# Even DFT tables ahead of the odd ones, and half of the odd ones issued from ScalarE

## The chip, the cores and the metric

The kernel runs on one core of a Trainium2 chip. The metric is the device time of one execution in microseconds (us): the median over several timed runs. Beside these there is one profiled execution, from which every row of the profile comes.

Engines are named as in the profile: PE (TensorE's matmuls), PEld (its weight loads), DVE (VectorE), ACT (ScalarE), POOL (GpSimd) and SP (SyncE, which computes nothing here and issues DMAs). SPq and ACTq are the DMA-issuing instructions of SP and ScalarE. L259 is line 259 of the kernel.

## The reference

`x` has shape 8 x 3136 x 256. All is float32 at the interface; the weights arrive as 64-bit floats, which the kernel narrows itself.

```python
X = np.fft.fft(x, axis=1)           # over the 3136 positions
X = np.fft.fft(X, axis=2)           # over the 256 features
x = X.real                          # float32

h  = np.maximum(x @ w_in, 0.0)      # w_in: 256 x 1024
hp = h padded with one zero row before and after each sequence
conv_out = conv_w[0] * hp[:, 0:S] + conv_w[1] * hp[:, 1:S+1] + conv_w[2] * hp[:, 2:S+2]
gate = 1 / (1 + np.exp(-conv_out))
out  = (h * gate) @ w_out           # w_out: 1024 x 256
```

## The kernel before

**Stages.** The Fourier transform over positions is made of matmuls with tables of cosines and sines. Symmetry is used first: `x[n]` and its mirror positions, and the quarters of the sequence, are added and subtracted on VectorE (the "fold", lines 156 to 194), so that the matmuls contract over 98 or 99 partitions only. The even output frequencies need the *even tables* (`tabs[0]`, tile `tab2`: cosine and sine, four columns of the fold, 393 frequencies each, 1.2 MB); the odd frequencies need the *odd tables* (`tabs[1]`, tile `tab4`: cosine and sine, 196 frequencies each for two columns, 0.3 MB) and, for the other two columns, the even tables again, with `w` scaled by a *turn* (`turn`, a cosine and a sine per partition, line 286). The transform over features is folded into `w_in` on PE (`G`, line 717). Then the FFN runs in steps of one sequence, one of four chunks of frequencies and one of eight blocks of 128 hidden units: two products on PE, ReLU sums and the convolution's taps on DVE and ACT, sigmoid on ACT, the gate on POOL and DVE, and the product with `w_out` on PE, which collects over the eight blocks.

**Order.** The order of the instructions on each engine is written out by hand. Sequence 0 is transformed alone at the start (the run-up); the transforms of sequences 1 to 7 are spread over the FFN steps of the sequence before. The change touches the run-up only.

**The run-up, as far as it matters.**

- *x of sequence 0* comes in two halves (`load_ops`, from line 109): one plain transfer from SP (line 118), four mirrored gathers from POOL (line 131), and for the second half three single-row transfers from ScalarE (line 125). A transfer is held back by a trick: POOL writes one element of the destination (`memset`, line 117) behind earlier work in its queue, and the transfer has to wait for that write.
- *Turn tables*: four transfers of 4-byte elements from ScalarE (line 286). Behind them ScalarE computes `turn[:, 2]` (line 697), which waits for them.
- *Odd tables* (`load_odd`, lines 268 to 280): for each of cosine and sine two transfers of 48 rows (one for the even and one for the odd partitions), one of two rows and one of the last row; eight in all from SP, held by a memset at line 698 that stands in POOL's queue behind the eight gathers.
- *Even tables* (`load_even`, lines 254 to 266): two transfers of 48 partitions, one of two, one of one, from SP behind the odd tables.
- Then, from SP too: the four blocks of `w_in` (line 651, tile `raw`) with the feature tables `dm` between them.
- *ScalarE* makes the scaled copies `rt` of the fold (`scaled`, line 216; four when the first half of x is folded, four when the second is), corrects a row of the odd tables (`mend_row`, line 294) and writes the negated and mirrored copies of both odd tables (`mirror_tables`, line 300).
- *PE* runs eight matmuls of 512 columns whose results nobody reads (`keep_on`, tiles `pb` and `pa`), then four units of the odd frequencies in turns, a quarter of each at a time (tiles `po<-tab,w` with the odd tables, `po<-tab,rt` with the even ones), then the units of the even frequencies.
- *VectorE* narrows the first block of `w_in` (lines 617 to 635) after the fold, then combines PE's results (lines 383 to 416).

A product takes 98 partitions of a table, and 99 where the fold's last column (`q == 3`) brings an extra row. In that extra row the odd tables hold zeros for the column with index 0 and a row of values for the column with index 1.

```python
for i in range(4):
    for j, u in enumerate(odds):
        u.part(i)
```

`dma_start` only issues; completion is reported through a semaphore, on which the reading instruction waits. The framework gives each transfer issued from SP or ScalarE one of eight such counters in turn, and makes a transfer wait until the one before it on the same counter has landed.

Of the kernel before, what the change touches and what calls it, by code (L numbers as in the profile page):

```python
# [30 lines left out]
NQ = 8  # L31
# [5 lines left out]
def kernel(  # L37
# [10 lines left out]
    nc = tc.nc  # L48
# [5 lines left out]
    NP = Q4 // NQ  # L54
    KR = NP + 1
    HQ = NQ // 2
    NK = M + 1
    HE = Q4 // 2 + 1
    HO = Q4 // 2
    QO = HO // 2  # L60
# [179 lines left out]
    tabs = [const.tile([P, 2, HQ, HE], F32, name="tab2"), const.tile([P, 4, 2, QO], F32, name="tab4")]  # L240
# [10 lines left out]
    MR = NP // 2 // 16 * 16  # L251
    assert NP == 2 * MR + 2

    def load_even():

        to = tabs[0].rearrange("p s q i -> p s (q i)")
        n = HQ * HE
        for i in range(2):
            nc.sync.dma_start(out=to[i:2 * MR:2], in_=dft_seq[0:MR, 0:2, HQ * i:HQ * (i + 1)]  # L259
                              .rearrange("p s q i -> p s (q i)"))  # L260
        nc.sync.dma_start(out=to[2 * MR:NP], in_=bass.AP(
            tensor=dft_seq.tensor, offset=dft_seq.offset + MR * 4 * NQ * HE,
            ap=[[n, 2], [NQ * HE, 2], [1, n]]))
        nc.sync.dma_start(out=to[NP:KR], in_=bass.AP(
            tensor=dft_seq.tensor, offset=dft_seq.offset + (NP * 4 * NQ - HQ + 2) * HE,
            ap=[[n, 1], [NQ * HE, 2], [1, n]]))

    def load_odd(eng):

        def at_(p, s, q):  # L270
            return dft_seq.offset + ((p * 4 + 2 + s) * NQ + q) * HE
        for s in range(2):
            for i in range(2):
                eng.dma_start(out=tabs[1][i:2 * MR:2, s], in_=bass.AP(
                    tensor=dft_seq.tensor, offset=at_(0, s, HQ * i + 1),
                    ap=[[4 * NQ * HE, MR], [2 * HE, 2], [1, QO]]))
            eng.dma_start(out=tabs[1][2 * MR:NP, s], in_=bass.AP(
                tensor=dft_seq.tensor, offset=at_(MR, s, 1), ap=[[HQ * HE, 2], [2 * HE, 2], [1, QO]]))
            eng.dma_start(out=tabs[1][NP:KR, s], in_=bass.AP(
                tensor=dft_seq.tensor, offset=at_(NP, s, -1), ap=[[2 * HE, 1], [2 * HE, 2], [1, QO]]))  # L280

    def load_turn(eng):

# [411 lines left out]

    load_turn(nc.scalar)
    act(turn[0:NP, 2], turn[0:NP, 1], AF.Copy, scale=-1.0)
    nc.gpsimd.memset(tabs[1][0:1, 0, 0, 0:1], 0.0)
    load_odd(nc.sync)
    load_even()  # L700
    w_in[0].load(nc.sync)
    nc.sync.dma_start(out=dm, in_=dft_dim[:, :, 0:2])
    for i in (1, 2, 3):
# [209 lines left out]
    p = psd.tile([P, 512], F32, name="pd", tag="pd")  # L913
# [200 lines left out]
```

## Time and profile before

| what | us |
|---|---|
| timed runs, median of 3 | 1200.08 (1199.71 to 1200.8) |
| the profiled execution's own time | 1194.98 |
| its span, first to last instruction | 1193.2 |
| PE busy | 1152.5 |
| DVE busy | 1134.9 |
| ACT busy | 899.6 |
| first 100 us: PE busy, DVE busy | 74.95, 79.83 |
| from 100 us on, of 1093.0: PE busy, DVE busy | 1077.55, 1055.03 |

A row of the profile's timeline gives start, duration, engine, line, operation, destination<-source, shapes and count, and in brackets the time the engine stood idle before it and what ended that. Rows of the chain of waits give start, duration and what the end of the program hung on at that time; followed back from the last instruction, the chain runs through the run-up. Times are from the start of the span. The mean of a core's granted TensorE clock over the span was 0.995 of full speed.

### The profile page before, as it was taken

What the parts mean: (1) busy time and instruction counts of PE and PEld (TensorE: products, weight loads), DVE (VectorE), ACT (ScalarE), POOL (GpSimd) and SP (SyncE); (2) the same over time, 40 slices, a digit from 0 to 9 for tenths busy, and PEclk for the clock granted to TensorE, in tenths of its full rate; (3) what the DMA queues carried; (4) which work ended last, traced back from release to release, by engine and by line L of the source; (5) the groups of instructions that cost most, each with busy time, mean ns of one, the idle gap of its engine ahead of it and who ended that gap; (6) DMA issues with size and microseconds to landing.
All of it is one profiled execution on the core that took longest, in us unless ns stands there. A gap on an engine that the chain in (4) does not pass through costs nothing.

```text
span 1193.2 us, 15532 instructions
## 1 busy us (share of the span) xinstructions
PE 1152.5 (97%) x4836; PEld 890.9 (75%) x4836; DVE 1134.9 (95%) x1693; ACT 899.6 (75%) x1937; POOL 405.5 (34%) x476
## 2 busy tenths in 40 slices
PE   3899999999999999999999999999999999999998
PEld 1766777678876787777778777777778777777776
DVE  6799999999999999999999999999999998999996
ACT  2377767787777777778786877888787777888885
POOL 5235524524253423344423242242312233222222
PEclk9899999999999999999999999999999999999999
DMA  7622232311032120211121020310001100110001
GB/s 179 200 17 75 77 41 74 89 40 57 13 108 59 55 61 30 73 54 61 47 75 51 15 81 27 89 47 27 27 16 39 32 27 28 47 34 27 27 27 31
DMA packets 70723, 65.16 MB, mean 55 GB/s; under 512 B 28563, under 2 KB 58535, under 8 KB 70641
## 3 DMA queue, kind: packets, MB, share of 16 engines
q1 hardware_dynamic: 64583, 51.05, 15.4%
q0 software_dynamic: 5120, 12.85, 3.7%
q8 instruction: 38, 0.62, 0.2%
q10 hardware_dynamic: 938, 0.28, 0.1%
q14 instruction: 44, 0.36, 0.1%
HBM read 38.40 MB, written 25.74 MB: 54 GB/s over the span
## 4 chain that ended last, share of the span: by engine, by line
PE 72%; DVE 16%; issue 4%; ACT 4%; DMA 2%; POOL 1%; SPq 0%; DVEq 0%; ACTq 0%; POOLq 0%
PE po L92 46%; PE pb L92 11%; PE pa L92 10%; DVE g L806 7%; PE pd L92 5%; DVE h L795 3%; DVE g L830 2%; POOL xh L131 1%; DMA tab<-dft_seq_dram 1%; ACT nb L784 1%; ACT g L821 1%; DMA out_dram<-os 1%; ACT os L854 1%; DVE w L194 1%; DMA xh<-in_x_dram 0%
## 5 line engine op out<-in xcount | busy, mean ns | idle before, releaser
L92 PE MATMUL po<-wout,g 128*128 128x256 f32 x3072 | 709.8, 381 | 10.8 <-DVE g L830 10.2
L92 PEld LDWEIGHTS po<-wout,g 128*128 128x128 f32 x3072 | 577.6, 190 | 166.3 <-DVE g L830 48.4
L806 DVE SCALAR_TENSOR_TENSOR g<-h,cw,g 128x770 f32<-128x770 f32 (+1 forms) x512 | 564.8, 1103 | 4.1 <-ACT g L801 0.9
L829 POOL TENSOR_TENSOR g<-g,h 128x385 f32<-128x385 f32 (+2 forms) x256 | 265.1, 1036 | 727.5 <-ACT g L821 550.2
L821 ACT ACTIVATE g<-g 128x385 f32<-128x385 f32 (+4 forms) x512 | 245.2, 531 | 167.9 <-DVE g L806 167.2
L784 ACT ACTIVATE nb<-pb 128x386 f32<-128x386 f32 (+2 forms) x494 | 218.6, 497 | 68.3 <-PE pb L92 66.8
L795 DVE CUSTOM_DVE_ANT_0 h<-pa,nb 128x386 f32<-128x386 f32 (+2 forms) x503 | 260.0, 556 | 1.7 <-POOL h L762 1.7
L801 ACT ACTIVATE g<-h,cw 128x770 f32<-128x770 f32 (+1 forms) x256 | 244.2, 954 | 0.0
L92 PE MATMUL pb<-qt,G 127*128 127x387 f32 (+2 forms) x512 | 214.6, 500 | 1.8 <-ACT nb L784 0.8
L92 PE MATMUL pa<-pt,G 128*128 128x387 f32 (+2 forms) x512 | 212.2, 495 | 0.3 <-ACT pa L748 0.3
L748 ACT ACTIVATE pa<-eb,ge 128x387 f32<-128x387 f32 (+2 forms) x256 | 155.3, 607 | 1.6 <-DVE h L795 1.0
L92 PEld LDWEIGHTS pa<-pt,G 128*128 128x128 f32 x512 | 97.2, 190 | 74.4 <-issue 18.1
L830 DVE TENSOR_TENSOR g<-g,h 128x385 f32<-128x385 f32 (+2 forms) x256 | 148.2, 579 | 3.4 <-ACT g L821 3.4
L131 POOL DMA_INDIRECT xh<-in_x_dram,idx x64 | 101.9, 1592 | 13.0 <-issue 9.7
L92 PE MATMUL pd<-tab,w 98*128 98x197 f32 (+2 forms) x448 | 98.5, 318 | 1.0 <-DVE w L194 1.0
L92 PEld LDWEIGHTS pb<-qt,G 127*128 127x128 f32 x512 | 91.1, 190 | 8.1 <-ACT G L717 2.0
L92 PEld LDWEIGHTS pd<-tab,w 98*128 98x128 f32 (+1 forms) x448 | 81.9, 191 | 10.8 <-issue 1.6
L854 ACT COPY os<-po 128x256 f32<-128x256 f32 x196 | 57.5, 398 | 8.7 <-DMA out_dram<-os 5.3
L156 DVE TENSOR_TENSOR xh<-xh 98x1020 f32<-98x1020 f32 (+1 forms) x32 | 39.4, 1234 | 4.0 <-DMA xh<-in_x_dram,idx 4.0
L167 DVE TENSOR_TENSOR xh<-xh 98x1024 f32<-98x1024 f32 (+1 forms) x32 | 39.9, 1246 | 0.1
L178 POOL COPY w<-xh 98x4 f32<-98x4 f32 (+1 forms) x32 | 26.9, 842 | 7.3 <-DVE xh L172 3.7
L193 DVE TENSOR_TENSOR w<-xh 98x508 f32<-98x508 f32 (+1 forms) x32 | 22.3, 698 | 0.1
(136 smaller groups left out, 376.9 us busy)
## 6 DMA issues: line engine op xcount, KB each, us to landing
out_dram<-os SPq DMA_DIRECT2D x192, 128.0 KB
xh<-in_x_dram SPq DMA_DIRECT2D x16, 784.0 KB
eb<-ed SPq DMA_DIRECT2D x16, 193.5 KB
raw<-in_moe_w_in_dram SPq DMA_DIRECT2D x4, 512.0 KB
raw<-in_moe_w_out_dram SPq DMA_DIRECT2D x1, 2048.0 KB
eb<-ed SPq DMA_DIRECT2D x8, 209.0 KB
eb<-ed SPq DMA_DIRECT2D x7, 193.0 KB
tab<-dft_seq_dram SPq DMA_DIRECT2D x2, 589.5 KB
```

The costliest lines, as they stand in the source:

```text
L92: nc.tensor.matmul(o, l, r, start=start, stop=stop, skip_group_check=True)
L131: nc.gpsimd.indirect_dma_start(out=xh[b, h][0:NP, 7 - m].rearrange("p q d -> p (q d)"), out_offset=None, in_=bass.AP(tensor=x.tensor, offs ...
L167: vt(flat(to, to + 2), flat(0, 2), flat(2, 4), op=op)
L748: act(pa[s][:, 0:n], eb[b, c], AF.Copy, scale=ge[:, f:f + 1])
L784: act(nb[s][:, i, cols], p[:, cols], AF.Copy, scale=-1.0 if i else 1.0)
L795: nc.vector._custom_dve(TENSOR_ADD_SAT, out=to, in0=a[:, cols], in1=c[:, i, cols], s0=BIG, s1=0.0)
L801: act(gs[s], hs[s][:, 0:n], AF.Copy, scale=cw[:, 0, s[2]:s[2] + 1])
L806: stt(out=g, in0=h[:, k:k + n], scalar=cw[:, k, f:f + 1], in1=g, op0=ALU.mult, op1=ALU.add)
L821: act(gs[s][:, c], gs[s][:, c], AF.Sigmoid)
L829: gt(g[:, p], g[:, p], h[:, p], op=ALU.mult)
L830: vt(g[:, v], g[:, v], h[:, v], op=ALU.mult)
L854: nc.scalar.copy(out=osb[:, j % 2], in_=pt[:, j % 2])
```

## The change

The order of the table loads in SP's queue is turned round: the even tables come right behind the second half of x, held by a memset of `tabs[0]`; the odd tables follow. `load_odd` now loads one of the two odd tables per call: the sine (`s = 1`) is issued from ScalarE's queue, behind the computation of `turn[:, 2]`, and the cosine (`s = 0`) from SP's queue behind the even tables. The extra row of both odd tables comes in one transfer with the sine, for the column with index 1 alone; the zeros of the column with index 0 are written by POOL (three partitions from 96 on; the loads then overwrite the first two of these). Seven transfers of odd tables take the place of eight, and three memsets that of one. What is computed stays the same.

```diff
-    def load_odd(eng):
-
-        def at_(p, s, q):
+    def load_odd(eng, s):
+
+        def at_(p, q):
             return dft_seq.offset + ((p * 4 + 2 + s) * NQ + q) * HE
-        for s in range(2):
-            for i in range(2):
-                eng.dma_start(out=tabs[1][i:2 * MR:2, s], in_=bass.AP(
-                    tensor=dft_seq.tensor, offset=at_(0, s, HQ * i + 1),
-                    ap=[[4 * NQ * HE, MR], [2 * HE, 2], [1, QO]]))
-            eng.dma_start(out=tabs[1][2 * MR:NP, s], in_=bass.AP(
-                tensor=dft_seq.tensor, offset=at_(MR, s, 1), ap=[[HQ * HE, 2], [2 * HE, 2], [1, QO]]))
-            eng.dma_start(out=tabs[1][NP:KR, s], in_=bass.AP(
-                tensor=dft_seq.tensor, offset=at_(NP, s, -1), ap=[[2 * HE, 1], [2 * HE, 2], [1, QO]]))
+        for i in range(2):
+            eng.dma_start(out=tabs[1][i:2 * MR:2, s], in_=bass.AP(
+                tensor=dft_seq.tensor, offset=at_(0, HQ * i + 1), ap=[[4 * NQ * HE, MR], [2 * HE, 2], [1, QO]]))
+        eng.dma_start(out=tabs[1][2 * MR:NP, s], in_=bass.AP(
+            tensor=dft_seq.tensor, offset=at_(MR, 1), ap=[[HQ * HE, 2], [2 * HE, 2], [1, QO]]))
+        if s:
+            eng.dma_start(out=tabs[1][NP:KR, 0:2, 1], in_=bass.AP(
+                tensor=dft_seq.tensor, offset=dft_seq.offset + ((NP * 4 + 2) * NQ + 1) * HE,
+                ap=[[HE, 1], [NQ * HE, 2], [1, QO]]))
...
     load_turn(nc.scalar)
     act(turn[0:NP, 2], turn[0:NP, 1], AF.Copy, scale=-1.0)
-    nc.gpsimd.memset(tabs[1][0:1, 0, 0, 0:1], 0.0)
-    load_odd(nc.sync)
+    nc.gpsimd.memset(tabs[0][0:1, 0, 0, 0:1], 0.0)
+    nc.gpsimd.memset(tabs[1][0:1, 1, 0, 0:1], 0.0)
+    nc.gpsimd.memset(tabs[1][96:KR, 0:2, 0], 0.0)
+    load_odd(nc.scalar, 1)
     load_even()
+    load_odd(nc.sync, 0)
     w_in[0].load(nc.sync)
```

## The prediction

> **What bounds the kernel now.** I read the page first, then the chain of waits over the first 120 us, the queue waits of SP, the timeline of the first 60 us, and last the windows and the DMA view around one gap. The span, and the busy time of each engine:
>
> ```profile
> span 1193.2 us, 15532 instructions
> PE 1152.5 (97%) x4836; PEld 890.9 (75%) x4836; DVE 1134.9 (95%) x1693; ACT 899.6 (75%) x1937; POOL 405.5 (34%) x476
> tab<-dft_seq_dram SPq DMA_DIRECT2D x2, 589.5 KB
> ```
>
> PE and DVE are both full from about 57 us to the end, and the change touches nothing there. It touches the run-up, where no engine is full. So the question is how many microseconds the run-up gets shorter; the rest follows it at a fixed distance. The chain of waits (start, duration, what):
>
> ```profile
> 13.49 4.61 DMA tab<-dft_seq_dram
> 18.12 0.62 SPq L274
> ...
> 20.80 0.62 SPq L259
> 21.46 0.60 SPq L259
> 22.11 7.66 DMA tab<-dft_seq_dram
> 29.90 10.60 PE po L92 x46
> 40.50 2.29 issue
> ```
>
> The odd tables (L274) are issued from 13.49, the even ones (L259) only from 20.80, and PE starts its run of 46 matmul passes at 29.90, right behind the even tables' landing (22.11 + 7.66 = 29.77). Why the even tables are issued so late stands in SP's own waits:
>
> ```profile
> SPq L274 <- DMA tab<-dft_seq_dram: 1.4, 1, 1.4
> SPq L277 <- DMA xh<-in_x_dram: 0.4, 1, 0.4
> ```
>
> In the built programs each hardware DMA carries one of eight completion counters, handed out in turn, and a ninth DMA waits until the first user of its counter has landed. So the fifth odd transfer stood until the first was in (13.49 + 4.61 = 18.10), and the third until the second half of x was in (it went out at 15.31, below). The timeline of what runs beside this:
>
> ```profile
> 13.38 0.09 POOL L698 MEMSET tab<- 1x1 f32 x1
> 13.52 1.40 POOL L873 MEMSET qt<- 32x1569 f32 x1
> ...
> 15.31 0.70 SPq L277 DMA_DIRECT2D tab<-dft_seq_dram  x1
> ...
> 16.45 7.84 PE L92 MATMUL pb<-w 98*128 98x512 f32 x12 [9.63 <-POOL w L178]
> ...
> 17.04 0.20 ACT L697 ACTIVATE turn<-turn 98x2 f32<-98x2 f32 x1
> ...
> 18.94 2.34 DVE L156 TENSOR_TENSOR xh<-xh 99x1020 f32<-99x1020 f32 x2
> ...
> 23.25 0.43 SPq L651 DMA_DIRECT2D raw<-in_moe_w_in_dram  x1
> ...
> 24.05 1.71 ACT L216 ACTIVATE rt<-w,turn 98x256 f32<-98x256 f32 x4 [5.13 <-POOL w L199]
> ...
> 25.78 0.80 ACT L294 ACTIVATE tab<-tab,half 2x196 f32<-2x196 f32 x2
> 25.84 0.49 PE L92 MATMUL po<-tab,w 98*128 98x196 f32 x2
> ...
> 26.61 1.19 ACT L300 ACTIVATE tab<-tab 99x196 f32<-99x196 f32 x4
> ...
> 29.90 1.65 PE L92 MATMUL po<-tab,rt 98*128 98x197 f32 x4 [3.56 <-DMA tab<-dft_seq_dram]
> ...
> 31.29 0.43 DVE L617 TENSOR_SCALAR win<-raw 128x512 int32<-128x512 int32 x1 [3.56 <-DMA raw<-in_moe_w_in_dram]
> ...
> 34.59 0.69 DVE L635 SCALAR_TENSOR_TENSOR win<-raw,win 128x512 f32<-128x512 f32 x1
> ...
> 38.80 0.32 ACT L379 COPY as<-po 128x196 f32<-128x196 f32 x1 [11.00 <-PE po L92]
> ```
>
> PE does two passes on the odd tables at 25.84, then stands 3.56 us for the even ones; everything else it needs (ScalarE's scaled copies at L216, the mended and mirrored odd tables at L294 and L300) is ready by 27.80. The windows (length, then busy time and count of PE, PEld, DVE, ACT, POOL; granted clock, DMA share, GB/s) show a second price of that gap:
>
> ```profile
> 26.34:29.90 3.56, 0.00 (x1) 0.03 (x1) 1.36 (x3) 1.43 (x5) 1.30 (x2) 0.76 1.00 202
> 29.90:35.02 5.12, 5.12 (x16) 5.12 (x17) 3.52 (x7) 0.00 (x0) 0.00 (x0) 0.50 0.97 352
> 35.02:40.50 5.48, 5.48 (x32) 5.16 (x30) 1.52 (x5) 0.97 (x3) 0.00 (x0) 1.00 0.01 4
> ```
>
> Until 35.02 the clock is at half: 16 passes take 5.12 us (0.32 each); the other 30 take 5.48 us (0.18 each).
>
> **The change, part by part.** *Even tables first.* Their hold is the memset that now stands where the odd tables' stood, so the first is issued at 13.49. The built program names the counters: the second even transfer waits for the second half of x, as L277 did (15.31), the two small ones for transfers long landed. In the trace, first issue to landing of all that PE needs took 29.77 - 20.80 = 8.97 us. What is new is that the tail of x still moves:
>
> ```profile
> q0 software_dynamic: 76, 0.14, 24.3%
> ...
> q1 hardware_dynamic: 312, 1.41, 98.8%
> ```
>
> The first row is x's mirrored rows from 15.2 to 18 us, 0.14 MB; the second SP's queue from 22 to 28 us, 1.41 MB in 6 us, 0.235 MB/us. So the tail costs 0.6 us: even tables landed at 13.49 + 8.97 + 0.6 = 23.1 (22.5 if the tail costs nothing), before PE gets to them at 26.3.
>
> *Odd tables, SP's half.* The built program puts a catch here: the second of its three transfers takes the counter of the second even one and waits for that to land (23.1); the two-row one goes behind it, and then w_in. Issue at 23.1 and 23.7. From issue to landing: 4.61 us in the first chain row, beside the tail of x; on a free queue about 2.5 by this row of the DMA view from 18 to 20.8 us, in which the four odd transfers issued from 18.12 have moved their 0.15 MB:
>
> ```profile
> q1 hardware_dynamic: 223, 0.15, 24.4%
> ```
>
> At 23 us the queue is free, so 2.5: landed at 26.2; bound 28.3.
>
> *Odd tables, ScalarE's half.* Four issues in ScalarE's queue behind L697 (17.24), at 0.6 to 0.7 each as SP's, 2.6 in all. The third takes the counter of the first even transfer, so ScalarE stands until that has landed: its 0.60 MB are half of the even data, so 0.60 / 0.235 = 2.6 us before the rest, and half the tail's cost, 20.2 (bound: with the rest, 23.1). Behind it in ScalarE's order wait L216 (two sets of four, 1.71 each), L294, L300, and with these PE. Release at 20.2, last issue at 21.5, first L216 set to 23.4, the second at 24.05 as before, because it waits for POOL. Cost nothing; from 21 on each microsecond would show.
>
> *Turn tables.* Their second transfer now waits for x's first half instead of a small weight; L697 moves by 0.7 at most, covered by the same slack. *Memsets.* Two more ahead of L873 on POOL: 0.09, and 392 elements at L873's rate, 0.35. The clock-keeping matmuls at 16.45 move by 0.44, and as part of that falls in half clock, PE reaches the tables at 26.1 instead of 25.84.
>
> *One transfer fewer, w_in earlier.* The first w_in block goes out at 24.4 instead of 23.25, but onto an empty queue: 0.52 MB at 0.235 MB/us and 2 us of latency, landed at 28.7 against 31.29. VectorE's narrowing takes 35.28 - 31.29 = 3.99, so done at 32.7, in time for PE's first finished unit (38.80 less 6 is 32.8). If it again took the 8.0 us it took before, it would come 3.6 late: a bound.
>
> *The sum.* L294 starts at 26.2 instead of 25.78, so L300 ends at 28.2. PE's first round, 12 passes at 0.18 from 26.1, ends at 28.2 too; the other 36 passes take 6.4 and end at 34.6 instead of 40.50: 5.9 us gained, 3.6 of them the gap and 2.3 the half clock. From there each step waits for the one before it on PE, ACT, DVE or POOL, and w_out and the next x are issued by the same steps, so all keep their distance. One thing does not:
>
> ```profile
> 24.78:28.19 3.41, 1.56 (x5) 0.57 (x3) 2.89 (x5) 2.96 (x9) 1.30 (x2) 1.00 1.02 227
> ...
> 38.43:41.84 3.41, 2.07 (x12) 1.75 (x11) 2.51 (x8) 1.08 (x4) 0.00 (x0) 1.00 0.00 0
> 41.84:45.26 3.42, 2.47 (x28) 2.00 (x29) 3.11 (x9) 2.74 (x8) 0.43 (x1) 1.00 0.35 68
> ...
> 48.67:52.08 3.41, 3.16 (x17) 2.32 (x16) 3.27 (x8) 0.91 (x3) 2.63 (x3) 1.00 0.95 294
> 52.08:55.50 3.42, 2.96 (x6) 1.45 (x5) 3.21 (x8) 1.75 (x5) 0.57 (x5) 0.50 0.65 157
> ```
>
> The clock changes on a grid of 3.41 us. A window with PE 1.56 us busy was followed by half clock, one with 2.07 was not, but one with 3.16 was: much of that is one-column matmuls, so busy time alone doesn't tell. That half window (52.08) fell on the step into the FFN. The work now moves 5.9 us along the grid, so such windows fall elsewhere: up to 1.7 us lost (a window's work at half speed), or, if the one at 52 goes, at most half of its 2.96 won, of which VectorE, 3.21 busy there, leaves perhaps 1. I take 0.4 lost. Gain 5.5: the profiled execution's own 1194.98 (span 1193.2) becomes 1189.5. The three timed runs lie 5.1 above it; kept, that gives 1194.6.
>
> The Trainium skill, page "TensorE: Matmul & The Clock Gate", Part 1, says that the window runs freely and that the gate closes after an idle window. The trace disagrees on the second: the window that closed it was 46% busy. By the page alone a wait of 1 or 2 us inside a window would cost no clock; I keep the row.
>
> **Rivals.** *Late odd tables.* SP's odd half and w_in stand behind the even landing. At the bounds (landing 28.3, or w_in at 32.4) L300 ends at 30.3 or VectorE is 3.6 late, PE ends at 36.7 to 38.4 with a half window: gain 2.1 to 3.8, about 1197.1. For it: the wait is certain, only its end is not. Against: the queue is empty by then.
>
> *x's tail starved.* VectorE takes the last mirrored rows at 20.1 (second of the two at 18.94). If a whole table transfer passes on each DMA engine before x's next rows, 0.60 MB at 0.235 is 2.6 us, the tail ends near 20.6 instead of 18, and near 23.2 behind both: VectorE, L216, L300 and PE 0.5 to 3 us late, the last 0.4 of them no news beside L294's own start at 26.2: gain 2.8 to 5.4. The Trainium skill, "DMA: Bandwidth & Descriptors", section "Queues, rings and completion order", states such a rule: an engine drains a whole packet of one ring before it turns to the next. The row from 15.2 to 18 shows both queues moving, but against short odd rows. Time about 1196.0.
>
> *Slower: the even tables crawl.* If x's tail and the table halve each other's rate all the way, 2 x 8.97 puts the landing at 31.4; SP's odd transfers land at 34.5, L300 ends at 36.5, PE at 42.9 or, with a half window, 44.6: 2.4 to 4.1 slower, 1203. It decides from a landing at 29.0 on (27.3 with a half window): 3.1 to the odd landing, 2.0 for L294 and L300 and 6.4 of passes then reach 40.5 again. Against it: only 0.14 MB of x is left.
>
> *It does nothing measurable.* The gap closes but the half windows and VectorE take back all but 2 us: 1198 to 1201.
>
> **How the numbers follow.** Forecast 0.58 (own range 1193.0 to 1195.9: gain 4.2 to 7.1); late odd tables 0.18; tail starved 0.08; nothing 0.09; slower 0.07. A change under 0.2% (2.4 us) can't be told from none here: below 1197.7 is faster. Faster 0.58 + 0.08 + 0.14 of the second case = 0.80; same 0.12 with the rest of that case; slower 0.08, the crawl and an edge of the fourth. The range takes the forecast's low end and most of the two middle cases: 1192.9 to 1198.4.
>
> **What would show it.** Right: L259 at 13.5, PE from 26.1 to about 34.6 without a gap over 0.5 us and the clock at 1.00 throughout, L617 at about 28.7, ScalarE's third issue released near 20.2, and every later step 5 to 6 us earlier. Wrong: L156's second start past 20.1, L294 past 27, L216's second set past 24.5, or PE waiting at L92 for odd instead of even tables.

## The result, and the profile after

The changed kernel took 1189.1 us (median of 5 executions, 1188.7 to 1193.96) against 1200.8 (1199.71 to 1201.39): the medians differ by 11.7 us. The ratio on record for the two sets of executions is 0.9932, with a 95% interval from 0.9909 to 0.9956; the bare quotient of the medians would be 0.9903. The forecast was 1194.6, with a range from 1192.9 to 1198.4. So the kernel became faster, as forecast, but by 11.7 us instead of 5.5, and the median lies below the range.

The profiled execution of the changed kernel is not one like that median: it took 1193.79 us. Its span, and its chain of waits in the run-up:

```profile
span 1192.0 us, 15535 instructions
...
24.94 8.27 PE po L92 x48
33.21 2.29 issue
35.50 0.88 PE pd L92 x16
36.38 8.35 PE po L92 x32
44.72 1.58 PE pd L92 x2
46.30 5.43 PE po L92 x16
```

The tables are gone from the chain. PE's 48 passes follow the clock-keeping matmuls without a gap and end at 33.21; before, they ended at 40.50. That is 7.3 us, yet the span is only 1.2 us shorter. The timeline shows the loads and what waits for them:

```profile
13.41 1.38 SPq L259 DMA_DIRECT2D tab<-dft_seq_dram  x2
...
16.04 6.03 SPq L273 DMA_DIRECT2D tab<-dft_seq_dram  x2
...
17.48 2.34 DVE L156 TENSOR_TENSOR xh<-xh 99x1020 f32<-99x1020 f32 x2
...
19.43 0.71 ACTq L275 DMA_DIRECT2D tab<-dft_seq_dram  x1
...
20.96 3.32 ACT L216 ACTIVATE rt<-w,turn 98x256 f32<-98x256 f32 x8
...
22.47 0.67 SPq L275 DMA_DIRECT2D tab<-dft_seq_dram  x1
...
24.38 0.80 ACT L294 ACTIVATE tab<-tab,half 2x196 f32<-2x196 f32 x2
24.78 0.49 PE L92 MATMUL po<-tab,w 98*128 98x196 f32 x2
...
25.21 1.20 ACT L300 ACTIVATE tab<-tab 99x196 f32<-99x196 f32 x4
...
27.25 0.43 DVE L617 TENSOR_SCALAR win<-raw 128x512 int32<-128x512 int32 x1 [0.98 <-DMA raw<-in_moe_w_in_dram]
```

SP stands between its two L273 transfers (16.04 + 6.03) for the counter of the second even transfer, and ScalarE until 19.43 for that of the first; in this execution both waits end before anyone needs what is behind them. Where the 7.3 us went stands in the windows (length, then busy time and count of PE, PEld, DVE, ACT, POOL; granted clock, DMA share, GB/s):

```profile
30.18:33.59 3.41, 3.03 (x18) 2.71 (x16) 2.57 (x7) 0.97 (x3) 0.00 (x0) 1.00 0.53 201
33.59:37.01 3.42, 1.51 (x22) 1.04 (x23) 3.35 (x10) 1.96 (x5) 0.00 (x0) 1.00 0.08 15
37.01:40.42 3.41, 3.41 (x14) 3.41 (x14) 1.97 (x6) 2.00 (x5) 2.69 (x5) 0.50 0.88 314
40.42:43.83 3.41, 3.41 (x14) 3.41 (x14) 3.27 (x7) 0.33 (x1) 2.75 (x3) 0.50 1.03 359
43.83:47.25 3.42, 3.42 (x10) 1.89 (x9) 2.39 (x6) 0.48 (x1) 1.19 (x5) 0.50 0.59 177
47.25:50.66 3.41, 3.41 (x10) 2.88 (x11) 2.78 (x5) 0.53 (x2) 0.00 (x0) 0.50 0.64 186
50.66:54.07 3.41, 2.95 (x6) 1.51 (x5) 0.00 (x0) 1.56 (x4) 0.00 (x0) 0.50 0.96 203
```

The next gap of PE, the 2.29 us behind the odd units from 33.21 on, now lies with 1.91 us inside one window of the clock's grid (33.59:37.01). That window is 1.51 us busy, and the clock then stays at half for five windows, 17.07 us. In the profile of before the same gap (from 40.50 on) was cut near its middle by the grid (38.43:41.84 with 2.07 busy, 41.84:45.26 with 2.47), and the clock held. The passes of the even units, which before took 4.85 us,

```profile
43.60 4.85 PE L92 MATMUL po<-tab,w 99*128 99x99 f32 x32
```

now take 8.35, and the first FFN products start at 52.19 instead of 53.54. (The row merges 32 passes and names the shape of the first; half of them have 98 or 99 columns, half 196 or 197.)

So the two profiled executions differ in two things: the order of the tables, and where the grid cut a gap. If the timed ones differ in the same way, their clocks must tell it. All five executions of the changed kernel have a mean granted clock on record: 1188.7, 1188.77 and 1189.1 us at 0.998; 1193.79 at 0.992 and 1193.96 at 0.994. For the five of before no clock is on record.

### The profile page after: what moved, and what is told of

It reads as the page before. It is cut to its first block, busy times and chain, and to the rows that moved or that the text cites. A ratio compares the mean times of both kernels' runs of the same rounds, so it can differ in the third digit from the quotient of the medians.

```text
span 1192.0 us, 15535 instructions
## 1 busy us (share of the span) xinstructions
PE 1155.9 (97%) x4836; PEld 893.5 (75%) x4836; DVE 1134.8 (95%) x1693; ACT 899.0 (75%) x1937; POOL 402.5 (34%) x478
## 4 chain that ended last, share of the span: by engine, by line
PE 75%; DVE 17%; issue 3%; ACT 3%; POOL 1%; DMA 0%; DVEq 0%; ACTq 0%; SPq 0%; POOLq 0%
PE po L92 47%; PE pb L92 12%; PE pa L92 11%; DVE g L809 8%; PE pd L92 5%; DVE h L798 3%; DVE g L833 2%; POOL xh L131 1%; ACT nb L787 1%; DVE w L194 1%; DMA out_dram<-os 0%; ACT g L824 0%; ACT os L857 0%; DVE xh L172 0%; ACT rt L220 0%
```

## The experiments

**Theory and rivals.** Clock grid: each kernel has a time at full clock, and on top a cost that depends on where the grid falls; the tables' order moves the first, and the 11.7 us compare executions that fell differently. Rival: the two groups have nothing to do with the clock (transfers, or the profile itself), and the order is worth 11 us.

### 1 and 2. Both kernels again

No edit.

> The kernel before, unchanged. Theory (clock grid): the granted TensorE clock changes on a free-running grid of 3.41 us, and where the 2.3 us gap of PE behind the odd units falls in that grid decides whether the clock stays at half for up to 17 us after it. So executions fall into two groups some 5 us apart: near 1195 with a mean clock of about 0.995, and near 1200 with 0.990 to 0.992; within a group the spread is under 1 us. Rival (transfers): the 1195 of the profiled execution against 1200 of the timed ones comes from the profile or from DMA, so the mean clock is the same 0.995 in all of them.

> The changed kernel, unchanged. Clock grid: two groups, near 1188.8 with clock 0.998 and near 1193.9 with 0.992 to 0.994, both seen. Against the kernel before, group by group: 1195 to 1188.8 and 1200.3 to 1193.9, so 6.2 to 6.4 us, what the tables' order alone is worth (forecast 5.5 to 5.9). Rival (transfers): no such pairing of time and clock, the gain 11 us.

The kernel before: 12 executions from 1192.16 to 1202.66, with clocks from 0.999 down to 0.988. The changed one: 12 from 1188.51 to 1195.44, clocks 1.000 to 0.992; only 2 of them in the lower group (up to 1189.24), the others from 1192.71 on. With the executions of before that were measured beside the later experiments there are 76 of before (its first five, without a clock on record, left out) and, with the first five, 17 of after. Times follow the clock: by a straight line through each set, 0.90 to 0.91 us for each 0.001 of mean clock, and at full clock 1190.2 us before and 1187.6 after. Medians: 1197.8 and 1193.2. The theory's pairing of time and clock holds, but the kernel before doesn't fall into two tight groups as expected, and the 6.2 to 6.4 us between groups that were expected can't be read off. It has two places for half clock. Behind the wait for the even tables the profiles show it; that it also comes behind the odd units is inferred, and no profile caught such an execution. A mean clock of 0.987 over 1200 us means some 31 us at half, more than the 3.4 to 6.8 us that the profiles show behind the wait, and experiment 4 takes most of it away. So its times spread over 11 us, and its best, 1191.48, lies below the "1195 group".

The first comparison had 3 of 5 executions of after in the lower group, where the 12 later ones had 2, and 5 of before all at 1199.7 or more, where 24 of the 76 later ones are. Five of five there would be a chance of 0.3% if each execution fell by itself, so something else may have been different in that session; what, the runs don't show. 4.6 us between the large sets is the better figure (95% interval by resampling the executions 2.8 to 8.2), and a rough one: the 12 executions of before here have a median of 1194.57, the 29 measured beside the experiments of the same session 1197.85.

The second profile of the changed kernel also shows the catch that the prediction named:

```profile
23.54 0.67 SPq L275 DMA_DIRECT2D tab<-dft_seq_dram  x1
...
25.64 0.80 ACT L294 ACTIVATE tab<-tab,half 2x196 f32<-2x196 f32 x2 [0.67 <-DMA tab<-dft_seq_dram]
...
26.47 1.17 ACT L300 ACTIVATE tab<-tab 99x196 f32<-99x196 f32 x4
27.70 0.30 PEld L92 LDWEIGHTS po<-tab,w 98*128 98x128 f32 x2 [0.75 <-ACT tab L300]
27.70 0.60 PE L92 MATMUL po<-tab,w 98*128 98x196 f32 x2 [0.43 <-ACT tab L300]
```

Here SP's odd half is late by 0.67 us for ScalarE, and PE waits 0.43 for the mirrored copies.

### 3 and 4. The gap behind the odd units filled, in both kernels

```diff
+    keep_on([idle] * 2)
     mend_row(0, half)
```

> The changed kernel with two more of the clock-keeping matmuls (512 columns, results unread) in PE's 2.3 us gap between the odd units and the feature unit; 2 x 0.86 us of work, so nothing real waits for them. Clock grid: no half clock after the gap, all executions near 1188.8, clock 0.997 to 0.998. Rival (transfers): still two groups, 1188.8 and 1193.9, in the old proportion.

> The kernel before with the same two matmuls in the same place (its first gap, the 3.56 us wait for the even tables, untouched). Clock grid: all executions near 1195 (1194 to 1196), clock 0.994 to 0.996; then the order of the tables is worth after_warm against this one, about 6 us. Rival (transfers): 1200 as before.

Changed kernel: 1187.71 (6 executions, 1187.38 to 1188.76, clocks 0.997 to 1.000). Kernel before: 1192.04 (12 executions, 1190.21 to 1193.32, 0.996 to 0.999), lower than the 1194 to 1196 expected. A likely reason, not tested: the profile of before that I took as the measure had a second half-clock window (52.08:55.50) and a late x. A spread of 11 us becomes 3, one of 7 becomes 1.4, with nothing touched but two matmuls whose results nobody reads. That shows the clock behind this gap as the cause of the spread; the rival falls. With the gap filled in both kernels the order of the tables is worth 1192.04 - 1187.71 = 4.3 us (95% interval by resampling 3.2 to 5.1), and the two ranges don't meet. The windows of the changed kernel with the gap filled:

```profile
31.70:35.12 3.42, 3.42 (x17) 2.78 (x16) 2.93 (x8) 0.97 (x3) 0.00 (x0) 1.00 0.38 147
35.12:38.53 3.41, 2.83 (x29) 1.70 (x28) 3.31 (x10) 2.58 (x7) 0.12 (x1) 1.00 0.27 35
38.53:41.94 3.41, 3.41 (x23) 3.18 (x22) 1.96 (x6) 1.72 (x4) 3.22 (x5) 1.00 0.99 357
41.94:45.36 3.42, 3.18 (x16) 2.38 (x16) 3.28 (x8) 0.64 (x2) 2.50 (x4) 1.00 0.96 335
45.36:48.77 3.41, 2.95 (x6) 1.52 (x6) 3.24 (x7) 1.74 (x4) 0.85 (x5) 0.50 0.53 149
```

One half-clock window is left, at 45.36, behind a window in which PE was busy 3.18 of 3.42 us; the kernel before with its gap filled still has half clock behind the wait for the even tables (27.15 to 33.98). In these two profiles PE's filler starts where the odd units end. Kernel before, then changed kernel:

```profile
span 1190.6 us, 15540 instructions
...
39.30 1.72 PE pb L92 x4
```

```profile
span 1185.9 us, 15543 instructions
...
34.07 1.72 PE pb L92 x4
```

The odd units end 5.2 us earlier and the span is 4.7 us shorter, so here nearly all of what the run-up gained reaches the end. (One such matmul shows as two records, hence x4.)

### 5 and 6. Order without the second queue, second queue without the order

Both on top of the filled gap. First, all odd transfers from SP behind the even ones:

```diff
-    load_odd(nc.scalar, 1)
     load_even()
     load_odd(nc.sync, 0)
+    load_odd(nc.sync, 1)
```

> after_warm with all seven odd transfers issued from SP behind the even tables, none from ScalarE: the order of the change without its second queue. Theory (the order is what pays): the odd transfers go out from about 19.4, when the first even one has landed and gives its counter back, the last at about 23, landed near 25.5; L300 ends near 27.5 to 28.3, PE waits up to 0.7 us more for it than in after_warm, so 1187.7 to 1188.6. Rival (the second queue pays): SP's four extra issues of 0.65 us push the odd tables and w_in 2.6 us back, 1190.3.

1187.81 (6 executions, 1187.33 to 1188.63): the same as with ScalarE's share, 1187.71. In its profile PE does wait for the odd tables, by more than the 0.7 us that were allowed for:

```profile
26.32 0.45 ACT L294 ACTIVATE tab<-tab,half 2x196 f32<-2x196 f32 x1 [1.23 <-DMA tab<-dft_seq_dram]
26.44 0.57 PE L92 MATMUL po<-tab,w 98*128 98x196 f32 x2 [2.14 <-DMA tab<-dft_seq_dram]
```

That profiled execution was the longest of the six (1188.63), 0.8 us above their median; whether the others had the wait too isn't known. Between the medians the second queue is worth 0.1 us, and by the ranges under 1.

Second, the old order, with the sine's half from ScalarE as in the changed kernel:

```diff
-    nc.gpsimd.memset(tabs[0][0:1, 0, 0, 0:1], 0.0)
+    nc.gpsimd.memset(tabs[1][0:1, 0, 0, 0:1], 0.0)
...
     load_odd(nc.scalar, 1)
+    load_odd(nc.sync, 0)
     load_even()
-    load_odd(nc.sync, 0)
```

(the hold of `tabs[0]` gives way to one of `tabs[1]`).

> after_warm with the old order on SP (odd tables ahead of the even ones), but the sine's half and the common last row issued from ScalarE: the second queue without the order. Theory (the order pays because it takes the even tables out from behind eight issues and their counters; fewer issues ahead do much of the same): first even transfer near 16, landed 8.97 later, 25.0, before or at PE's first need; 1187.7 to 1188.7. Rival (only the order pays): the even tables still land past 28 and PE stands about 3 us with half clock behind it, 1191 to 1192.

1188.47 (7 executions, 1187.25 to 1192.07, the longest at a clock of 0.996 where the others had 0.998): 3.6 of the 4.3 us. The timeline says why:

```profile
15.91 1.26 SPq L259 DMA_DIRECT2D tab<-dft_seq_dram  x2
...
25.93 0.57 PE L92 MATMUL po<-tab,w 98*128 98x196 f32 x2 [0.90 <-DMA tab<-dft_seq_dram]
26.33 0.86 PE L92 MATMUL po<-tab,rt 98*128 98x197 f32 x4
```

With three issues ahead instead of eight, and counters of transfers long landed, the two large even ones go out at 15.91 instead of 20.80 and are there when PE comes (the 0.90 us that it waits at 25.93 are for the odd tables; its passes on the even ones follow at 26.33 without a wait). What cost before was eight issues and a reused counter in front of the transfer that is longest on its way. Either part of the change takes that away; together they add little to each other.

### 7. The wait kept, the cooling taken away

The kernel before with both gaps filled:

```diff
             u.part(i)
+            if i == 0 and j == 0:
+                keep_on([idle] * 3)
...
+    keep_on([idle] * 2)
     mend_row(0, half)
```

> before_warm with three more clock-keeping matmuls (2.6 us) behind PE's first two passes on the odd tables, so that PE still waits for the even tables but doesn't cool down. Theory: the wait of 3.2 to 3.9 us costs its own length, which stays, and 1.5 to 2.3 us of half clock on the passes behind it, which goes: 1189.5 to 1190.5 against 1192.0. Rival (the half clock behind the gap is covered by VectorE's narrowing of w_in): no change, 1192.

1190.33 (9 executions, 1189.57 to 1191.4). PE's passes on the even tables still begin late, but at full clock:

```profile
26.17 0.49 PE L92 MATMUL po<-tab,w 98*128 98x196 f32 x2
26.50 2.74 PE L92 MATMUL pb<-w 98*128 98x512 f32 x6
29.08 0.86 PE L92 MATMUL po<-tab,rt 98*128 98x197 f32 x4
```

(Three matmuls, so x6.) So of the 4.3 us, 1.7 are the half clock behind the wait (1192.04 to 1190.33; 95% interval by resampling 1.0 to 2.4) and 2.6 the late start (to 1187.71; 1.6 to 3.2). In this profile PE goes from the filler to the even tables without a wait, so the filler may have run a little past their landing, and the wait alone may be a little less than 2.6. The two lines above, read at full clock (1190.2 and 1187.6), give the same 2.6.

### 8. One matmul more, before the FFN

```diff
     blocks(0)
+    keep_on([idle])
     w_in[2].narrow(0, 2)
```

on top of the filled gap.

> after_warm with one more such matmul between the products that make G and the first FFN products, where after_warm's profile still had one half-clock window (45.36 to 48.77). Theory: the last half window goes in most executions, 1186.5 to 1187.4. Rival (that stretch waits for VectorE and ScalarE, and the matmul of 0.9 us stands in the way): 1187.7 to 1188.6.

1188.69 (7 executions, 1187.85 to 1191.79): 1.0 us longer, as the rival had it. In the one profile that was taken the half-clock window (45.32 to 48.73) is still there, and it had begun before the filler ran:

```profile
47.48 1.64 PE L92 MATMUL pb<-w 98*128 98x512 f32 x2
```

So this filler could not have prevented it, and it cost about its own length.

### 9 and 10. What the gate looks at

One matmul in the gap instead of two, in the changed kernel:

```diff
+    keep_on([idle])
     mend_row(0, half)
```

> The changed kernel with one clock-keeping matmul (0.86 us) in the 2.3 us gap instead of two. Theory (the gate looks at how busy PE was in a 3.41 us window): the gap shrinks to 1.4 us, so every window that holds it has at least 2.0 us of work, above the 1.1 to 1.6 us after which the clock was seen to drop: all executions near 1188, as with two. Rival (only a gap filled nearly to the end will do, or the placing of the two matmuls acts in another way): executions at 1193 to 1195 remain, though fewer than 12 of 17.

12 executions, 5 of them from 1187.13 to 1189.19 with clocks of 0.998 to 1.000, 7 from 1191.8 to 1194.34 with 0.993 or 0.994; median 1191.87. The rival was right: one is not enough. My estimate that a window with 2.0 us of work holds the clock doesn't carry to this stretch, and where the mark lies is open: the one profile taken is of an execution at clock 1.000, so no window of an upper execution is known.

Three matmuls behind the first unit of the even frequencies, the gap left as it is:

```diff
         u.matmuls(0, 1)
+        if i == 1:
+            keep_on([idle] * 3)
         u.copy()
```

> The changed kernel with the 2.3 us gap left alone and three clock-keeping matmuls (2.6 us at full clock, 5.1 at half) behind the first unit of the even frequencies. Theory (the half clock lasts five windows because the even units' short passes, 99 and 197 columns behind 128-column weight loads, keep the gate's measure low): one window full of 512-column passes brings the clock back, half-clock time falls from 17 to 7 to 10 us, and the upper group moves from 1194.6 to about 1192 to 1193; the lower group pays up to 1.5 us, 1189 to 1190. Rival (the length is set by something else, transfers or time): half until near 54 as before, and the matmuls' 5.1 us on top, 1196 to 1199 in the upper group.

8 executions: 1188.01 to 1188.91 at clock 1.000, and 1190.87 to 1192.97 at 0.995 to 0.997. The windows of the profiled one, of the upper group:

```profile
33.50:36.91 3.41, 1.32 (x20) 0.85 (x21) 3.38 (x9) 1.77 (x5) 0.00 (x0) 1.00 0.20 46
36.91:40.32 3.41, 3.41 (x9) 1.93 (x9) 1.97 (x6) 2.19 (x5) 2.50 (x5) 0.50 0.85 295
40.32:43.74 3.42, 3.42 (x7) 1.80 (x6) 1.94 (x4) 0.00 (x0) 2.81 (x3) 0.50 1.03 370
43.74:47.15 3.41, 3.41 (x24) 3.16 (x22) 1.67 (x4) 0.32 (x1) 1.31 (x6) 1.00 0.58 177
```

The half clock lasts two windows instead of five, and that although 5 us of work at half clock were put in; the rival (half until near 54) falls. The window that brings the clock back (40.32:43.74) is as busy by the profile as the first two of the changed kernel (37.01:40.42 and 40.42:43.83) that don't; it holds 512-column matmuls in place of the even units' passes. So busy time alone doesn't bring the clock back. But neither does every short pass keep it down. In the kernel before, one window at half clock full of 196- and 197-column passes of the odd units, behind the same 128-column weight loads, was enough:

```profile
31.60:35.02 3.42, 3.42 (x12) 3.42 (x12) 3.21 (x7) 0.00 (x0) 0.00 (x0) 0.50 0.92 340
35.02:38.43 3.41, 3.41 (x21) 3.41 (x20) 0.27 (x1) 0.00 (x0) 0.00 (x0) 1.00 0.02 6
```

What the even units have and these have not is passes of 98 and 99 columns. That these keep the clock down fits all the rows, but is not tested. Nor would it explain the whole 17.07 us: from 44.73 on, in the third to the fifth window, PE does other products (of one row, of one column, and of 256 columns).

The lowest median is that of the changed kernel with the gap filled (experiment 3), 1187.71; the 1187.81 of experiment 5 can't be told from it.

## Why the prediction was wrong, point by point

- **The gap and the cooling behind it: right in kind, somewhat smaller in size.** PE ran from 24.78 to 33.21 without a break at full clock, 7.3 us ahead of before; the forecast was 5.9. About 1.1 of the 1.4 us of excess is x arriving earlier: VectorE's second fold step starts at 9.89 instead of 11.32 (rows below), and PE comes to the tables at 24.78 instead of 25.84. The kernel before, profiled again, had PE there at 25.00, so this is no part of the change. With the gap behind the odd units filled, the two terms of the forecast, 3.6 for the wait and 2.3 for the half clock, came out as 2.6 and 1.7 (experiment 7). The fold step before, and after:

```profile
11.32 1.22 DVE L156 TENSOR_TENSOR xh<-xh 98x1020 f32<-98x1020 f32 x1 [1.79 <-DMA xh<-in_x_dram,idx]
```

```profile
9.89 1.22 DVE L156 TENSOR_TENSOR xh<-xh 98x1020 f32<-98x1020 f32 x1 [0.15 <-DMA xh<-in_x_dram,idx]
```

- **SP's odd half behind the even landing: right as a mechanism, at the small end.** Its last issue came at 22.47 and 23.54 in the two profiles (forecast 23.7), L294 at 24.38 and 25.64 (26.2), PE's wait 0 and 0.43.
- **ScalarE's queue: right.** Its third issue came at 19.43 (forecast 20.2), and both sets of L216 were done at 24.28. That it buys nothing by itself is experiment 5: 1187.81 against 1187.71.
- **x's tail: not starved.** VectorE took the second half of x at 17.48 with no wait in front. The rival by which a whole table transfer passes first would have put a wait of up to 2.6 us there; no profile here shows it. The Trainium skill (page "DMA: Bandwidth & Descriptors", section "Queues, rings and completion order") lets an engine drain a whole packet of one ring before it turns to the next; that the packet is a whole transfer was the rival's reading.
- **The steps that failed** are "up to 1.7 us lost (a window's work at half speed)", of which it took 0.4, and the 5.1 us between the profiled and the timed executions, which it "kept". The first was mis-sized: once the clock drops in front of the even units it stays down for 17.07 us, and at 0.9 us for each 0.001 of mean clock that makes some 5 us between the two groups of the changed kernel. This is why the profiled execution took 1193.79 where 1189.5 was forecast for it. The second put the median wrong. It took for a constant of the measurement what was such a cost: the profiled execution of before ran at 0.995, and later executions of before at 1199 to 1201 ran at 0.988 to 0.991. The prediction added that cost to a kernel of which some executions have it and some do not, and the median of the first five is one that has not: 1189.1, near the 1189.5 from before the 5.1 were added.
- **Luck.** That three of the first five executions held the clock is luck: of the next twelve, two did. And that the median of all 17, 1193.2, lies in the forecast's range is luck too, because the 5.1 that was added stands for a cost of the kernel before, and happens to be as large as the 5 us between the changed kernel's groups.
- **What the change is worth** against the forecast of 5.5: 4.3 with the gap filled in both, 4.6 between the large sets, 2.6 by the two lines read at full clock, 11.7 in the first five against five. The first three lie inside the gain of the range, 1.7 to 7.2.
- **The gate's rule: the row was right to keep.** The Trainium skill's page "TensorE: Matmul & The Clock Gate", Part 1, lets the gate close after an idle window; here windows with 1.51 and 1.32 us of work closed it. In experiment 4's profile one with 1.65 us closed it (23.73 to 27.15), and in experiment 5's one with 1.81 us left it open (22.48 to 25.89). That the window runs freely (the same section) the traces bear out: the drop comes at 28.19, 30.36 and 27.15 us after the start in three profiles in which PE reached the tables at 25.84, 25.00 and 24.89 and then waited for the even ones. The latter two:

```profile
30.36:33.78 3.42, 3.42 (x13) 3.42 (x12) 2.77 (x6) 0.00 (x0) 0.00 (x0) 0.50 0.95 350
```

```profile
27.15:30.56 3.41, 2.00 (x6) 2.03 (x7) 0.50 (x2) 0.00 (x0) 0.00 (x0) 0.50 1.03 338
```

## What to carry to other kernels

Before two versions are compared by a few microseconds, look at the granted clock of every execution: where a short idle time of PE can fall inside or across a window of the clock's grid, a handful of executions measure the grid. Fill such a gap with work nobody waits for, in both versions, and then compare; the filler must be long enough (two matmuls did it here, one did not), and best stands where PE is idle anyway: in front of the FFN one cost 1.0 us. Behind a drop it can still pay: experiment 10's took 5 us of PE's time, and the upper group went from between 1192.7 and 1195.4 to between 1190.9 and 1193.0. In a DMA queue put first what takes longest to arrive and is needed first, and count the issues and the reused counters ahead of it: either part of this change alone, with the gap filled, brought 4.2 and 3.6 of the 4.3 us.

## What the hardware showed that I had not expected

The clock did not come back by PE being busy. With the passes of the even units (half of 98 or 99 columns, half of 196 or 197, each behind a weight load of 128) PE was marked busy for the whole of two windows (37.01 to 43.83) and the clock stayed at half, for five windows in all; three 512-column matmuls among them ended it after two, and one window full of the odd units' 196 and 197 columns ended it too. Nor did the clock always hold with PE busy: the window before the drop at 45.36 in experiment 3 was busy for 3.18 of 3.42 us, 1.2 of them with one-column products. And the spread that follows, 1191.48 to 1202.66 us over 76 executions of one kernel, is nearly 1% of the time. As far as the profiles show it comes out of the first 60 us: the changed kernel's clock is at 1.00 from 54.07 on, that of before from 55.50 on.
